# Batch 0 of a tuned attention and gating kernel: q loaded like k and transposed by TensorE, statistics of v summed beside ScalarE's copies, and a new written order

## The chip, the cores and the metric

The kernel runs on one core of a Trainium2 chip. Its time is the device time of one execution, in microseconds (us), and the median of several runs is what is compared. The profile and the trace come from one further execution under the hardware profiler, whose own time and span are in the table below. The engines are called as in the profile: PE (TensorE), DVE (VectorE), ACT (ScalarE), POOL (GpSimd) and SP, the queue that issues every transfer here.

## What is computed

```python
def _attn_ref(q, k, v, phi):                     # q, k, v: 8 x 8 x 576 x 64, phi: 8 x 8 x 576 x 32
    a = np.exp(phi - np.max(phi, axis=2, keepdims=True))
    a = a / (np.sum(a, axis=2, keepdims=True) + 1e-09)
    k_m = np.einsum('bhsm,bhsd->bhmd', a, k)
    v_m = np.einsum('bhsm,bhsd->bhmd', a, v)
    scores = 1.0 / np.sqrt(64) * np.matmul(q, k_m.transpose(0, 1, 3, 2))
    attn = np.exp(scores - np.max(scores, axis=-1, keepdims=True))
    attn = attn / (np.sum(attn, axis=-1, keepdims=True) + 1e-09)
    return np.matmul(attn, v_m)

def _moe_ref(x, w_in, w_spatial, b_spatial, w_out):   # x: 8 x 576 x 512, heads side by side
    h = np.maximum(x @ w_in, 0.0)
    u, v = h[..., :512], h[..., 512:]
    mu = np.mean(v, axis=-1, keepdims=True)
    var = np.mean((v - mu) ** 2, axis=-1, keepdims=True)
    v_n = (v - mu) / np.sqrt(var + 1e-06)
    v_s = np.einsum('ts,bsd->btd', w_spatial, v_n) + b_spatial[None, :, None]
    return (u * v_s) @ w_out
```

The weights of the second half come as 64-bit floats, which the kernel turns into 32-bit ones with integer operations ("decoding" below).

## The kernel before, in words

The eight batches are worked off one after the other, each as a set of stages that overlap with those of the next batch. Every stage is a Python generator, and each `yield` ends one step of it. Two strings set the order in which the steps are written: `START` for the weights and the beginning of batch 0 and batch 1, `PLAN` for one round of the steady state. A letter names the stage, the digit its part, a prime the batch ahead, `*2` a repetition. Since the order is written out by hand (`manual_schedule`), every engine works its own instructions off in that order, and an instruction that waits holds up all that stand behind it on its engine.

The stages of a batch: `P` (`memory_weights`) loads phi, takes column maxima (`half`, `mx`, `cm`), the exponential and the sums `es`. `K` (`memories`) loads k and v into `kv_sb`, multiplies them with the exponentials (`kvm`), divides (`den`, `kmn`, `vmn`) and transposes (`tk`, `tv`, `kT`, `vT`). `Q` (`queries`) loads q and makes `qT`. `S` (`scores`) makes the scores `sc`, brings them to rows with four VectorE transposes (`sm`), takes the softmax, turns it back (`aT`) and splits it into a rounded high part `ah` and a rest `al`. `M` (`products`) makes v_m times one half of `w_in` (`mp`; `M0` for u, `M1` for v) and splits it into `mh` and `ml`. `U` (`units`, tile `pu`) and `V` (`gate`, tile `pv`) multiply `ah`, `al` with `mh`, `ml`; `V` also normalizes v and splits it into `vh`, `vl`. `G` (`spatial`, tile `ps`) and `O` (`project`, tile `po`) are the two large multiplications behind.

The stages of the weights: `D` loads `w_in` in eight transfers (`raw`), `L0`, `L1` decode the half for u and `E0`, `E1` the half for v, each in two tiles of 128 rows by twice 512 words. `W`, `T`, `B` load `w_spatial` and its bias, transpose it into `wt` and split it into `wth`, `wtl` (and `ws1`, `ws2` for the last 64 rows). `X0` to `X3` load and decode `w_out`.

The set `ON_VECTOR` says what VectorE does. A `.add` or `.mul` of a decoding that is not in it goes to GpSimd in two instructions of 512 words each (for `.add`, with a conversion on ScalarE ahead). A rest (`ml...`, `wtl...`) that is not in it is made by a matmul with minus the identity into the same bank and a ScalarE copy; one that is in it is a VectorE subtraction. A name `es3` stands for the sums `es` of batch 3, on VectorE if it is in the set and on GpSimd if not.

Before the change q of every batch comes in pieces of 32 numbers (128 bytes) that lie so in the tile that four VectorE transposes of 32x32 blocks make `qT` of them. Means and variances of v are taken by VectorE's `bn_stats` and `bn_aggr`, and GpSimd makes 1/sqrt(var) and the shift of them.

## Time and profile before

| | before |
|---|---|
| median of 3 runs | 435.25 us (434.84 to 436.11) |
| profiled execution, its own time | 435.84 us |
| its span, first to last instruction | 434.1 us |
| PE busy | 400.4 us, 92% of the span |
| PE weight loads (beside the matmuls) | 333.1 us, 77% |
| DVE busy | 294.9 us, 68% |
| ACT busy | 223.0 us, 51% |
| POOL busy | 74.0 us, 17% |
| mean granted clock of TensorE | 0.971 |

An engine's busy share is an average over the start, in which transfers and decoding keep the engines waiting for each other, and a long stretch in which TensorE works without a break. The clock is given as a share of full speed: 1.00 is 2.4 GHz, 0.50 is 1.2 GHz.

### The profile page before, as it was taken

How to read it: one execution, taken by the hardware profiler on the slowest of the kernel's cores; microseconds unless marked ns; L12 is line 12 of the kernel's file. 1: busy time of each engine (PE TensorE's matmuls, PEld its weight loads, DVE VectorE, ACT ScalarE, POOL GpSimd, SP SyncE). 2: the span in 40 equal slices, each digit the busy share in tenths (PEclk: the TensorE clock that was granted, in tenths of full speed). 3: DMA queues.
4: the chain of work that ended last, by engine and by line, in shares of the span. 5: the costliest groups of instructions: out<-in, count | busy, mean ns of one | idle time of the engine just before them, and what ended most of it. 6: DMA issues, size and time to landing. Idle time of an engine off the chain costs nothing.

```text
span 434.1 us, 9211 instructions
## 1 busy us (share of the span) xinstructions
PE 400.4 (92%) x3815; PEld 333.1 (77%) x3815; DVE 294.9 (68%) x546; ACT 223.0 (51%) x427; POOL 74.0 (17%) x148
## 2 busy tenths in 40 slices
...
GB/s 292 405 192 360 123 57 99 271 0 149 208 181 2 72 179 210 47 24 113 204 142 2 112 176 203 16 73 132 210 68 24 98 2 2 2 74 23 2 2 121
DMA packets 94543, 50.69 MB, mean 117 GB/s; under 512 B 75491, under 2 KB 79587, under 8 KB 94501
## 3 DMA queue, kind: packets, MB, share of 16 engines
q1 hardware_dynamic: 94500, 50.10, 47.5%
...
## 4 chain that ended last, share of the span: by engine, by line
PE 87%; DVE 6%; DMA 4%; ACT 1%; issue 1%; SPq 0%; DVEq 0%; ACTq 0%
PE ps L634 28%; PE po L674 23%; PE pv L547 13%; PE pu L596 12%; PE kvm L371 4%; PE mp L517 4%; DMA raw<-in_moe_w_in_dram 2%; DMA w_rem<-in_moe_w_spatial_dram 2%; PE sc L455 2%; DVE power L206 1%; DVE win_sb L214 1%; DVE win_sb L219 1%; DVE qT L441 1%; DVE half L317 0%; DVE g L645 0%
## 5 line engine op out<-in xcount | busy, mean ns | idle before, releaser
L634 PE MATMUL ps<-wth,vh 128*128 128x288 f32 x256 | 57.8, 307 | 0.1
L559 POOL TENSOR_SCALAR rs<-mv 128x1 f32<-128x1 f32 (+1 forms) x40 | 10.1, 253 | 262.7 <-DVE mv L556 238.0
L634 PE MATMUL ps<-wth,vl 128*128 128x288 f32 x256 | 54.6, 295 | 0.0
L634 PE MATMUL ps<-wtl,vh 128*128 128x288 f32 x256 | 54.5, 294 | 0.0
L674 PE MATMUL po<-wol,gh 128*128 128x512 f32 x128 | 50.8, 397 | 0.0
L674 PE MATMUL po<-woh,gh 128*128 128x512 f32 x128 | 50.6, 395 | 0.0
L674 PE MATMUL po<-woh,gl 128*128 128x512 f32 x128 | 50.2, 392 | 0.0
L680 ACT COPY o<-po 128x512 f32<-128x512 f32 x36 | 21.2, 588 | 55.8 <-PE po L674 53.5
L634 PEld LDWEIGHTS ps<-wth,vh 128*128 128x128 f32 x256 | 40.4, 188 | 10.9 <-issue 5.9
L554 DVE BATCH_NORM_STATS2 st<-vr 128x6 f32<-128x512 f32 (+1 forms) x40 | 27.3, 682 | 29.8 <-ACT vr L551 29.6
L656 ACT CAST gh<-g 128x512 fp32r<-128x512 f32 x32 | 19.1, 620 | 49.1 <-DVE g L645 49.1
L634 PEld LDWEIGHTS ps<-wtl,vh 128*128 128x128 f32 x256 | 41.2, 188 | 0.0
L634 PEld LDWEIGHTS ps<-wth,vl 128*128 128x128 f32 x256 | 41.0, 188 | 0.0
L605 ACT ACTIVATE u<-pu 128x576 f32<-128x576 f32 x32 | 20.2, 659 | 30.6 <-PE pu L596 30.2
L569 ACT ACTIVATE vr<-vr,sh,rs 128x512 f32<-128x512 f32 (+1 forms) x40 | 31.9, 817 | 5.4 <-POOL sh L564 5.4
L547 PE MATMUL pv<-mh,al 128*128 128x512 f32 (+1 forms) x80 | 31.6, 395 | 0.0
L547 PE MATMUL pv<-mh,ah 128*128 128x512 f32 (+1 forms) x80 | 31.6, 395 | 0.0
L547 PE MATMUL pv<-ml,ah 128*128 128x512 f32 (+1 forms) x80 | 31.6, 395 | 0.0
L658 DVE TENSOR_TENSOR grl<-g,grh 128x64 fp32r<-128x64 f32 x32 | 6.7, 213 | 36.3 <-ACT grh L656 36.3
L645 DVE TENSOR_TENSOR g<-u,ps 128x576 f32<-128x576 f32 x32 | 24.1, 752 | 9.7 <-PE ps L634 9.5
L596 PE MATMUL pu<-ah,mh 128*128 128x288 f32 x128 | 29.2, 309 | 0.0
L371 PE MATMUL kvm<-kv_sb,phi_sb 64*32 64x128 f32 x1152 | 23.3, 300 | 5.8 <-DMA kv_sb<-in_v_dram 5.0
...
## 6 DMA issues: line engine op xcount, KB each, us to landing
...
```

What stands on the lines that cost most here:

```text
L371: nc.tensor.matmul(kvm[r][32 * j : 32 * j + 32], phi_sb[halves[r], j, i, :], kv_sb[halves[r], j, :, i * D : (i + 1) * D], start=(i == 0), ...
L517: nc.tensor.matmul(mps[r][32 * j : 32 * j + 32, :], vT[D * r : D * r + D, 32 * j : 32 * j + 32], win_sb[D * r : D * r + D, j, cs], start=True,
L547: nc.tensor.matmul(pv, x[:, r, cs], m[:, r, DM:DFF], start=(n == 0), stop=(n == 5))
L554: nc.vector.bn_stats(st6, vr)
L569: nc.scalar.activation(vr, vr, AF.Identity, bias=sh, scale=rs)
L596: nc.tensor.matmul(pu[:, hf, 0:HALF], m[:, r, cs], a[:, r, hf * HALF : (hf + 1) * HALF], start=(n == 0), stop=(n == 5),)
L605: nc.scalar.activation(u[:, dt, :].rearrange("p (a s) -> p a s", a=2), pu[:, :, 0:HALF], AF.Relu)
L634: nc.tensor.matmul(ps[:, hf, 0:HALF], a, w[:, hf * HALF : (hf + 1) * HALF], start=(n == 0), stop=(n == len(ops) - 1),)
L645: nc.vector.tensor_tensor(g.rearrange("p (a s) -> p a s", a=2), u[:, dt, :].rearrange("p (a s) -> p a s", a=2), ps[:, :, 0:HALF], op=ALU.mult,
L656: nc.scalar.copy(hi, x)
L674: nc.tensor.matmul(po, a, w, start=(n == 0), stop=(n == 11))
L680: nc.scalar.copy(o, po)
```

## The change

Five things change. The first three are in batch 0 alone.

- q of batch 0 is loaded by one transfer in the layout of k (rows of 9 times 64 numbers, 2,304 bytes in one piece). TensorE transposes it in 24 pieces into five banks (`tq_0` to `tq_4`), and ScalarE copies these into `qT` with six instructions. VectorE's four transposes of batch 0 are gone.
- The columns of the scores of batch 0 come in another sequence by that, so the way back (`aT`) takes eight VectorE transposes in place of four, with a stride in what they write.
- v of batch 0: the ScalarE instruction that applies Relu also sums (`accum_out`); GpSimd makes plus and minus the mean of the sum; a ScalarE Square with minus the mean as bias sums the squares, and GpSimd makes variance, root and shift of it. `bn_stats` and `bn_aggr` of batch 0 are gone.
- `ON_VECTOR` is another set: `E0.mul`, `E1.add`, `E1.mul` go to GpSimd (and ScalarE), `L1.add`, `L1.mul` come to VectorE; the rests of `w_spatial` are named one by one, and some are now made by a matmul; the sums `es` of batches 4 to 7 go to GpSimd.
- `START` and `PLAN` are written in another order.

```diff
 START = """
-    D1 P W T3 P T3 B D0 T3 D0 T3 P*2 D1 T3 T2 L0 P E0 D1 T2*2 P T2 T3*2 P K P E0*2 L0 D1 P*2 K
...
+    W B T1 B P W P T1*2 W P D0 P T0 P*2 D0 P*2 T1 L0 P L0*2 W D0 D1 P L0 D0 D1 K L1*2 E0 P*2 K
...
 ON_VECTOR = set(
     """
-    es0 E0.add E0.mul E1.add E1.mul L0.add L0.mul ml000 wtl2 X0.add X1.add X1.mul X3.wol ml110
-    ml111 ml100 ml101 es2 es3 es4 es5 es6 es7
+    es0 E0.add ml010 L0.add L0.mul L1.add L1.mul wtl00 wtl0512 wtl1512 X0.add X0.mul X0.wol
+    X1.add X1.mul X2.add X2.wol ml111 ml100 ml101 es2 es3
     """.split()
...
-            tensor.matmul(x, minus, hi, start=False, stop=True, skip_group_check=True)
+            n = x.shape[0]
+            tensor.matmul(
+                x, minus[0:n, 0:n], hi, start=False, stop=True, skip_group_check=True
+            )
...
-                yield from low(f"wtl{si}" if cs.start == 0 else None, wtl[:, si, cs], part, hi)
+                yield from low(f"wtl{si}{cs.start}", wtl[:, si, cs], part, hi)
             else:
-                yield from low(None, ws2[0:SR, cs], part[0:SR], hi[0:SR])
+                yield from low(f"wtl{si}{cs.start}", ws2[0:SR, cs], part[0:SR], hi[0:SR])
...
     def queries(b, _):
+        if b == 0:
+            q_sb = one.tile([P, NJ, NX * D], F32, tag="q_sb", name="q_all")
+            nc.sync.dma_start(
+                q_sb, q[b].rearrange("(j r) (p i) d -> (r p) j (i d)", r=2, i=NX)
+            )
+            yield
+            qT = state["qT", b] = one.tile([P, H, HALF], F32, name="qT")
+            for j in range(NJ):
+                tq = bank(f"tq_{j}")
+                for n in range(4):
+                    cs = slice(n * P, (n + 1) * P)
+                    nc.tensor.transpose(tq[:, cs], q_sb[:, j, cs], ident)
+                yield
+                nc.scalar.copy(
+                    qT[:, 2 * j : 2 * j + 2, 0:256].rearrange("p r (i s) -> p r i s", s=64),
+                    tq.rearrange("p (i r s) -> p r i s", r=2, s=64),
+                )
+                yield
+            tq = bank("tq_4")
+
+            for j in range(NJ):
+                cs = slice(j * P, (j + 1) * P)
+                nc.tensor.transpose(tq[:, cs], q_sb[:, j, 7 * D :], ident)
+                nc.tensor.transpose(tq[0:D, cs], q_sb[:, j, 8 * D :], ident)
+            yield
+            for c in range(2):
+                rows = slice(D * c, D * c + D)
+                nc.scalar.copy(
+                    qT[rows, :, 256:],
+                    tq[rows].rearrange("p (h s) -> p h s", s=64)[:, :, 32 * c : 32 * c + 32],
+                )
+                yield
+            return
...
+                if b == 0:
+                    to = aT[:, r].rearrange("p (h x i) -> p i h x", x=32, i=NX)
+                    nc.vector.transpose(
+                        to[:, c:8:2], sm[:, r, c, 0:8].rearrange("p (i h) m -> p i h m", h=2)
+                    )
+                    nc.vector.transpose(to[:, 8, c], sm[:, r, c, 8])
...
+        if b == 0:
+
+            nc.scalar.activation(vr, pv, AF.Relu, accum_out=sums[:, 0:1])
+            yield
+            nc.gpsimd.tensor_scalar(sums[:, 1:2], sums[:, 0:1], -1.0 / DM, None, op0=ALU.mult)
+            nc.gpsimd.tensor_scalar(mv[:, 0:1], sums[:, 0:1], 1.0 / DM, None, op0=ALU.mult)
+            squares = vh[:, st, :] if st < NI else t1[0:SR]
+            nc.scalar.activation(
+                squares, vr, AF.Square, bias=sums[:, 1:2], accum_out=sums[:, 2:3]
+            )
+            yield
+            nc.gpsimd.tensor_scalar(
+                rs, sums[:, 2:3], 1.0 / DM, 1e-6, op0=ALU.mult, op1=ALU.add
+            )
+        else:
...
```

The built programs show where these instructions land. The first place is the queue of transfers (SP) from its start to the second phi, before:

```order
L174 DMA raw<-in_moe_w_in_dram 128x1024
L326 DMA phi_sb<-in_phi_dram 128x4x288
L256 DMA w_sb<-in_moe_w_spatial_dram 128x4x576
L257 DMA w_rem<-in_moe_w_spatial_dram 64x576
L259 DMA b_sb<-in_moe_b_spatial_dram 1x576 x2
L174 DMA raw<-in_moe_w_in_dram 128x1024 x4
L359 DMA kv_sb<-in_k_dram 128x4x576
L174 DMA raw<-in_moe_w_in_dram 128x1024
L359 DMA kv_sb<-in_v_dram 128x4x576
L174 DMA raw<-in_moe_w_in_dram 128x1024 x2
L432 DMA q_sb<-in_q_dram 32x72x32 x4
L326 DMA phi_sb<-in_phi_dram 128x4x288
```

And in the changed kernel:

```order
L260 DMA w_sb<-in_moe_w_spatial_dram 128x4x576
L261 DMA w_rem<-in_moe_w_spatial_dram 64x576
L263 DMA b_sb<-in_moe_b_spatial_dram 1x576 x2
L330 DMA phi_sb<-in_phi_dram 128x4x288
L178 DMA raw<-in_moe_w_in_dram 128x1024 x6
L363 DMA kv_sb<-in_k_dram 128x4x576
L363 DMA kv_sb<-in_v_dram 128x4x576
L434 DMA q_all<-in_q_dram 128x4x576
L178 DMA raw<-in_moe_w_in_dram 128x1024 x2
L330 DMA phi_sb<-in_phi_dram 128x4x288
```

`w_spatial` moved to the front, the four strided transfers of q became one, and the last two of the eight `raw` (those of `E1`) now stand behind q. Six `raw`, `w_spatial`, phi and k stand ahead of v in both.

The second place is TensorE from the transposes of batch 0's memories (`tk`) to its scores (`sc`), before:

```order
L283 MATMUL wt_308<-ident,w_dup 128x128 x4
L283 MATMUL wt_308<-ident,w_rem_dup 128x64
L411 MATMUL tk_317<-ident,kmn 128x128 x2
L416 MATMUL tv_325<-ident,vmn 128x128
L283 MATMUL wt_338<-ident,w_sb 128x128 x4
L283 MATMUL wt_338<-ident,w_rem 128x64
L455 MATMUL sc_0_0_344<-qT,kT 32x288
```

And in the changed kernel, where the eight pieces of `tq_4` end with six more like the last two rows, and the scores follow:

```order
L415 MATMUL tk_295<-ident,kmn 128x128 x2
L443 MATMUL tq_300<-ident,q_all 128x128 x4
L420 MATMUL tv_307<-ident,vmn 128x128
L443 MATMUL tq_312<-ident,q_all 128x128 x4
L159 MATMUL wt_190<-wth,minus 128x512
L443 MATMUL tq_324<-ident,q_all 128x128 x4
L443 MATMUL tq_332<-ident,q_all 128x128 x4
L454 MATMUL tq_338<-ident,q_all 128x128
L455 MATMUL tq_338<-ident,q_all 64x128
```

The transposes of q came in between `tk` and the scores, and two of the five transposes of `w_spatial` moved behind the scores.

The third place is VectorE around the reading of batch 0's scores, before:

```order
L206 SCALAR_TENSOR_TENSOR power<-raw,power 128x1024
L441 STREAM_TRANSPOSE qT<-q_sb 128x576 x4
L315 TENSOR_TENSOR half<-phi_sb 128x512
L317 TENSOR_TENSOR half<-half 128x4x64
L319 TENSOR_TENSOR mx<-half 128x128
L466 STREAM_TRANSPOSE sm<-sc_0_0_344 128x288
L466 STREAM_TRANSPOSE sm<-sc_0_1_345 128x288
L466 STREAM_TRANSPOSE sm<-sc_1_0_346 128x288
L466 STREAM_TRANSPOSE sm<-sc_1_1_347 128x288
L321 TENSOR_TENSOR mx<-mx,phi_sb 128x128
L472 TENSOR_REDUCE rmx<-sm 128x36
```

And in the changed kernel:

```order
L319 TENSOR_TENSOR half<-phi_sb 128x512
L321 TENSOR_TENSOR half<-half 128x4x64
L503 STREAM_TRANSPOSE sm<-sc_0_0_350 128x288
L323 TENSOR_TENSOR mx<-half 128x128
L503 STREAM_TRANSPOSE sm<-sc_0_1_351 128x288
L325 TENSOR_TENSOR mx<-mx,phi_sb 128x128
L503 STREAM_TRANSPOSE sm<-sc_1_0_352 128x288
L503 STREAM_TRANSPOSE sm<-sc_1_1_353 128x288
L341 TENSOR_REDUCE cm<-mt_382 128x2
L509 TENSOR_REDUCE rmx<-sm 128x36
L210 SCALAR_TENSOR_TENSOR power<-raw,power 128x1024
L512 TENSOR_TENSOR sm<-sm,rmx 128x1152
```

The four transposes of q are gone, fewer decoding steps stand ahead of the scores, and one of them (L210 of `E1`, L206 before) now stands inside the softmax.

## Rows read from the trace of the kernel before

**Rows 1.** Windows: start:end, us; busy us (instructions) by engine; PE clock; DMA share, GB/s.

```profile
0.00:57.44 57.44, 27.65 (x422) 16.37 (x422) 42.77 (x67) 27.79 (x50) 14.05 (x20) 0.79 0.95 259
57.77:434.10 376.33, 372.46 (x3394) 316.41 (x3392) 251.79 (x480) 194.89 (x378) 59.91 (x128) 1.00 0.41 95
```

**Rows 2.** Windows of 5 us inside the start; columns as in rows 1.

```profile
40.00:45.00 5.00, 3.48 (x35) 1.16 (x36) 4.93 (x9) 0.00 (x0) 3.20 (x3) 0.50 1.13 346
...
55.00:60.00 5.00, 5.00 (x133) 4.85 (x114) 4.91 (x14) 3.62 (x7) 0.15 (x1) 0.78 0.20 45
```

**Rows 3.** Timeline of DVE: start us, us, instruction, count [idle before].

```profile
29.66 1.21 DVE L206 SCALAR_TENSOR_TENSOR power<-raw,power 128x1024 int32<-128x1024 int32 x1
...
35.18 2.32 DVE L206 SCALAR_TENSOR_TENSOR power<-raw,power 128x1024 int32<-128x1024 int32 x1
37.43 2.75 DVE L441 STREAM_TRANSPOSE qT<-q_sb 128x576 f32<-128x576 f32 x4
...
43.35 1.56 DVE L466 STREAM_TRANSPOSE sm<-sc 128x288 f32<-128x288 f32 x4
...
51.44 0.68 DVE L162 TENSOR_TENSOR ws<-wt,ws 64x512 fp32r<-64x512 f32 x1
...
55.12 0.74 DVE L499 TENSOR_TENSOR al<-aT,ah 128x576 fp32r<-128x576 f32 x1
```

**Rows 4.** Timeline of PE in the start.

```profile
23.41 2.39 PE L371 MATMUL kvm<-kv_sb,phi_sb 64*32 64x128 f32 x80 [5.01 <-DMA kv_sb<-in_v_dram]
25.73 0.80 PE L157 MATMUL wt<-wth,minus 128*128 128x512 f32 x1
...
27.35 0.29 PE L383 MATMUL kvm<-ones,es 64*32 64x2 f32 x16
...
36.08 1.06 PE L283 MATMUL wt<-ident,w_sb 128*128 128x128 f32 x4
...
38.34 4.02 PE L455 MATMUL sc<-qT,kT 64*32 64x288 f32 x32 [0.91 <-DVE qT L441]
...
53.51 3.85 PE L371 MATMUL kvm<-kv_sb,phi_sb 64*32 64x128 f32 x135 [0.82 <-ACT ml L160]
...
57.77 0.42 PE L596 MATMUL pu<-ah,mh 128*128 128x288 f32 x2
```

**Rows 5.** Windows of 2 us around the end of the last `raw` transfers; columns as in rows 1.

```profile
22.00:24.00 2.00, 0.59 (x24) 0.62 (x32) 2.00 (x5) 2.00 (x3) 0.00 (x0) 1.00 1.04 392
...
26.00:28.00 2.00, 1.65 (x81) 1.12 (x81) 2.00 (x3) 1.44 (x2) 0.00 (x0) 1.00 0.84 127
```

**Rows 6.** Groups by line: shapes, count | busy us, mean ns of one | idle before.

```profile
L569 ACT ACTIVATE vr<-vr,sh,rs 128x512 f32<-128x512 f32 (+1 forms) x40 | 31.9, 817 | 5.4 <-POOL sh L564 5.4
...
L551 ACT ACTIVATE vr<-pv 128x512 f32<-128x512 f32 (+1 forms) x40 | 23.2, 594 | 8.4 <-PE pv L547 8.3
...
L398 ACT ACTIVATE kmn<-kvm,den 128x128 f32<-128x128 f32 x16 | 5.7, 362 | 0.5 <-DVE den L394 0.5
```

**Rows 7.** Timeline of POOL in the start.

```profile
34.80 3.84 POOL L212 TENSOR_TENSOR win_sb<-win_sb,raw 128x512 f32<-128x512 f32 x2 [32.35 <-ACT raw L204]
...
40.21 3.07 POOL L222 TENSOR_TENSOR win_sb<-win_sb,power 128x512 f32<-128x512 f32 x2
```

**Rows 8.** Chain that ended last: start us, us, engine, tile, line, count.

```profile
57.93 1.59 PE pu L596 x12
59.52 2.80 PE pv L547 x12
...
71.60 1.13 PE sc L455 x32
72.73 1.78 PE ps L634 x12
74.51 1.88 PE mp L517 x32
...
106.62 0.99 PE kvm L371 x58
```

More of the change, by code (lines that the diff above doesn't have):

```diff
@@ new lines @@
+    L1*3 L0 P L1 Q T0 T1 E0 T1 L1 T1 T0 P E0 P D1 E0*3 D1 T0 T2 E0 T0 K L1 K*2 L0 K*3 W T2 L0 K
+    L0 Q E1 K*2 Q*2 K Q P' T2 E0 Q T0 E1 T2 Q*5 T0 Q S P'*2 S P' S P' S*2 E1 P'*2 S T4 T2 E1*2
+    T2 T4 M0 X1 E1 P' M0 P' S E1 T2 K' P' M0 T4 S K' T3 T4 X0 E1 M1 T4 M0*2 Q' T3 P' S M1 T4 M0
+    P' S*3 T3 M0 M1 S K' M1*2 S T3 S*2 T4 T3 P'*2 M1 T3 U3 S T3 U2 Q' P' X1 M1 X0 K' S*2 X0 X1
+    V0 X1 X0*2 K'' U2 X0 K' X1 K' X1 V0 K' U2 V0 X0 X1 X0 V1*2 K' X0 P'' U3 V2 V0 U3 V0 K'*2 X1
+    V2 V1 Q' K' V0 U0 V2 V1 V4 V1 V0 X0 V1 Q'*2 K' V1 Q' U0 V4 U0 U1 V3 U1 V3 U1 V2 G1 V4 V2 X0
@@ L39 @@
+    X1 S' G1 V3 S' X3 V2 V4*2 G0 S'*2 V4 M1' V3 S' V4 V3*2 S' M0' G0 V2 G1 M1' X3 V4 M0' X3*2 V3
+    X3 S' G0 G1 P'' G0 M0' G1 X1*2 S' X3 X2 S' G2 G1 G0*2 G1 M1' P'' G1 G0 G2 M1' X3 G3 P'' G2
+    G1 X2 P'' K'' G3 X2*2 G0 G2 M0'*2 G2 P'' M1' P'' X2*2 G2 G3 P'' M0' G0 X2 O1 P'' X3*3 G3 X2
+    M1' M0' X2*2 P'' G3*2 X2 O3 X3 M1' G2 O2 O0 G3 S'*2 O3 S'*2 O2 O3 Q'' S'*4 O2 P'' G2 S'*2
+    P'' G3 O0 O3 O1 O2 G3 O0 G2 P''*2 O0 O1*2 P''
 """
 PLAN = """
-    P'*4 K' U0 V1 V0 K' U0 V2 U0 K' U2 V0 V1 U1 V1 V0 V2 V1 V2 K' V0 V4 U1 V1 V3 Q' K' V0 P'' V1
@@ L48 @@
+    V3 U3 Q' U2 V1 V4*2 K' V2 P'' K'*2 P'' V3 P'' K' P'' V3 V4 K' K'' U3 K' S' U2 U3 V2 V4 S' V3
+    S' V3 S'*2 G0 V4 G1 P'' M0' Q'' P'' M1' M0' S' V3 V2 S' M1'*2 G0 V4 G1 G0 V3 S' G1 V4 G0 P''
+    M1' S' M0' Q G1 G0 M1' G0 S' G1 S' M1' K'' P'' G0 S' Q'' G1 G0*2 M0' G2 G3 P'' G2 S' G3 G1*3
+    G2 G3 G2*3 M1' G3 O3 G2 S' G3 S'*2 O0 G3 S' O1 G3 O0 S' G3 P'' M0' S' O3 O0 G2 O0 G3 O1 O3
+    M0' O3 O4 G2 Q'' O2 M0' O1 O4 O1 V0' O2 O4*2 Q'' O2 V0' O2
 """
@@ L492, in scores @@
             for c in range(2):
[L493 to L495 removed]
+                if b == 0:
[5 more added lines that the diff above has]
+                else:
+                    nc.vector.transpose(
+                        aT[:, r].rearrange("p (i c x) -> p c i x", c=2, x=32)[:, c], sm[:, r, c]
+                    )
                 yield
```

37 lines of the change are left out of this document (8 added, 29 removed).

## The prediction

> **What bounds the kernel now.** I read the windows first, then the timelines of TensorE and VectorE in the start, then the chain. The reader is to see two regimes. From 57.77 us on TensorE is busy for 372.46 of the 376.33 us that are left, at full clock [rows 1], and what it does there are matmuls that the change does not touch. So the time is: the moment at which TensorE reaches its first `pu` matmul with all inputs there, plus the work that is left then. Up to 57.44 TensorE is busy for only 27.65 us, and VectorE for 42.77 [rows 1]; in the windows VectorE is full from 40 on while TensorE idles or runs at half clock [rows 2]. What ends last there is VectorE's queue. It decodes weights, makes the four transposes of q at 37.43, gets to the scores at 43.35 and to the first rest `al` at 55.12 [rows 3]. The scores themselves waited for those transposes: `sc` starts at 38.34 after an idle time that L441 ended [rows 4]. TensorE's first `pu` at 57.77 comes 2.65 behind `al`, because 135 `kvm` matmuls of batch 1 stood ahead of it at half clock, from 53.51 for 3.85 us [rows 4].
>
> So the question is when the scores of batch 0 are ready for VectorE, and how much VectorE does from there to `al`.
>
> **The start, step by step.** *Transfers.* Before v stand the same bytes in both orders, so v lands at 23.4 as now, where `kvm` starts [rows 4]. Behind it q, 1.18 MB, needs 3.0 us at the 392 GB/s of the window before the strided q and 9.3 at the 127 GB/s of the window in it [rows 5]. k and v, in the same layout, are the nearest rows: I take 3.0, so q is there at 26.4. Nothing asks for it before 28.7 (below), so its transfer is hidden; at the slow rate it would land at 32.7. The last two `raw` follow it, about 1.0 MB or 2.7 us more, at 29.1; VectorE comes to them (L187) later than that.
>
> *Memories.* The `kvm` group ran from 23.41 to 27.64, with an L157 matmul of 0.80 inside [rows 4] that is elsewhere now: 27.2. VectorE's `den` and two ScalarE `kmn` of 0.36 [rows 6] give `tk` at about 28.7.
>
> *Transposes of q.* Two queues run side by side. On ScalarE there stand, from `kmn` to the last q copy, six full-width copies (four of q, one `wth`, one `wtl`) and nine smaller ones. The copies of q write with a stride that no row shows; I price them as L551, 0.59, and the small ones as `kmn`, 0.36 [rows 6]: 27.9 + 6 x 0.59 + 9 x 0.36 = 34.7. On TensorE four groups of four transposes cost 1.06 each by the group of `wt` at 36.08 (half clock), one L157 0.80, and the eight of `tq_4` two groups [rows 4]: 28.7 + 4.2 + 0.8 + 2.1 = 35.8, and two copies of 0.36 behind: 36.5. At full clock TensorE is well ahead, and ScalarE's 34.7 decides. I take 35.4 for the first score matmul. Half of the scores cost 0.6 at full clock (1.13 for all [rows 8]) and twice that at half: VectorE reads them at 36.2, in place of 43.35. Bounds: 35.3 and 37.7.
>
> VectorE itself is free at about the same time. Behind `den` it has three decoding steps of 1.21 and five short ones, at most 0.68 each like the L162 [rows 3]: 27.7 + 3.6 + 3.4 = 34.7, or 37.3 if the two GpSimd operations of `E0.mul` shut it out for 1.3 each (below).
>
> *From the scores to `al`.* Before this took 55.12 - 43.35 = 11.8 us without a gap [rows 3]. Now one L206 of 1.21 comes in (the decoding step of `E1`), a subtraction L162 of 0.68 goes [rows 3], and the first `aT` pair becomes four transposes that write with a stride; I take 0.1 for it, and up to 0.7 if short pieces cost twice their share: 12.4. GpSimd comes on top. Its two additions at 34.80 took 3.84 us [rows 7], and the L206 that VectorE began at 35.18 took 2.32 in place of 1.21: as if it had stood still to 36.3, inside the pair, and then run [rows 3]. Now four such GpSimd operations of `E1` fall between the scores and `al`, and two VectorE instructions there read two SBUF tiles, L210 and L512. Each can lose one GpSimd operation, (3.84 - 1.21) / 2 = 1.3 without the lockout, so the bounds are 0 and 2.6. I take 1.6: 1.1 for L210, as before, and 0.5 for L512. So `al` starts at 36.2 + 12.4 + 1.6 = 50.2.
>
> That is also about when the other inputs come. `E1` now goes through ScalarE (behind the q copies: 35.4, three conversions of 1,024 words, each about twice a copy of 0.59, 38.8), GpSimd (3.84 + 3.07 [rows 7], 45.7), the last `mp` matmuls (a quarter of 32 that take 1.88 at full clock [rows 8], 0.9 at half), an `mh` copy of 0.59 and the hand-overs, 47.5; VectorE wants that `mh` for `ml`, just ahead of `al`, at 49.6. Cover: 2.1 us. If GpSimd is later than that, everything behind `ml` is late one for one.
>
> *First `pu`.* TensorE's queue has ahead of it 80 `kvm` matmuls of batch 1 (3.85 for 135 at half clock [rows 4], so 2.3), from the exponential of phi at about 48 (on ScalarE it is the sixth instruction behind that of the scores), and a last L157 that waits for three ScalarE instructions behind `ah`: 51.2. Before: 57.77.
>
> **The sum.** 51.2, plus the 376.33 left from the first `pu` on [rows 1], plus what moved behind it: the other 64 `kvm` matmuls and the sums, 1.1 (0.99 for 58 [rows 8]), and one rest of batch 1 by matmul, 0.25. The clock: before it is 0.50 up to 55 and 0.78 on average from 55 to 60 [rows 2], so it rose behind the `kvm` run that began at 53.51. Now that run begins at about 48 and I expect the rise between 51 and 53; at half clock the first `U` halves cost double (1.59 for two [rows 8]): 0.8, between 0 and 1.6. For small waits later 0.3. Sum 430.0 against the span of 434.1, 4.1 less. The profiled execution took 435.84, 1.7 more than its span, and lies 0.6 above the runs' median; 435.25 - 4.1 = **431.1**.
>
> **What I cost at nothing.** *Statistics.* Five `bn` pairs leave VectorE, which is no gain by itself: it is not what TensorE waits for there. ScalarE gets five Squares; with a bias they lie between L551's 0.59 and L569's 0.82 [rows 6], and the sums may add 0.2 to ten instructions. GpSimd makes five small operations per block in place of three. The cover: from the first ScalarE Relu, at 56.0, to the last `vh` stand 30 instructions, near 19 us by these rows and 16 as they overlap: 72.1. TensorE needs that `vh` after four `U`, five `V`, six pieces of `ps`, `sc` and `mp`: 6.4 + 7.0 + 4.8 + 1.1 + 1.9 [rows 8] and 1.5 for the rest behind 51.2 + 0.8, 74.7. Slack 2.6; without it, each us late costs one. *Transfers of batch 1.* Its q shares the tile of batch 0's q and waits for `tq_4` at 35.4 instead of VectorE at 40.2. *PLAN.* TensorE's rows of batches 1 to 7 come in almost the same order; `es4` to `es7` go to GpSimd, busy for 59.91 of 376.33 us [rows 1], two batches ahead of their use. If that cover failed, a batch would lose about two operations of 512 words, 3 us [rows 7].
>
> **Rivals.**
> - *`E1` is late.* The chain above breaks its 2.1 us of cover, because q's copies stand ahead of it on ScalarE and GpSimd is shut out too. Needs 5 us of lateness to eat 2.8 us of the gain: 434.0 to 436. Against it: GpSimd's four rows now sum to 6.9 with lockouts in them. 0.11.
> - *Statistics late.* ScalarE or GpSimd lose the 2.6 us of slack and 1 to 3 more: 432.5 to 434. For it: L569 waited 5.4 us for GpSimd's `sh` in all [rows 6], and GpSimd now has more to do ahead of it. 0.14.
> - *More is gained.* Scores at 35.3, no lockout, clock up at once: 36.2 - 35.3 + 1.6 + 0.8 = 3.3 less at the most, 427.8 to 429.3. 0.13.
> - *Slower: GpSimd shuts VectorE out.* Place: between the scores and `al`. By rows `E1`'s four GpSimd operations take 6.9 us, and `es` of batch 1 begins there too, some 3 us more. If VectorE stood for all 9.9 instead of 1.6, the time is 431.1 + 8.3 = 439.4; it is slower than before by over 0.3% from 7.1 of the 9.9 on. For it: the doubled L206. Against it: the transposes of q at 37.43 ran at 0.69 each beside GpSimd's pair, without such a jump, and most of the softmax reads one tile or a bank. 0.07. The Trainium skill has the rule behind it (SBUF — State Buffer, § Who interferes with whom): the port pair that VectorE and GpSimd share is locked for a whole instruction, and the loser blocks. The 2.32 us of L206 agrees with that.
>
> **How the numbers follow.** The forecast as summed, 429.3 to 432.5, has 0.55. A difference of 0.3% (1.3 us) is about what this measurement can tell from none: same is 433.9 to 436.6. Faster: 0.55 + 0.14 + 0.13 = 0.82; same 0.11; slower 0.07. The range leaves out the slow rival (0.07), most of late `E1` (0.09) and the end of the gain (0.04): 428.3 to 434.3.
>
> **What would show it.** In the new trace: v lands near 23.4 and q before 29; `tk` near 28.7; the scores' VectorE transposes near 36 with an idle time ahead of them that TensorE ends; L210 stretched by GpSimd; `al` near 50; the first `pu` near 51; no gap of TensorE behind that. I am wrong if `pu` comes after 55, if ScalarE's q copies cost much more than 0.6, if `ml` ahead of `al` waits for `mh`, or if TensorE waits for `vh` in the first `ps`.

## The result, and the profile after

The changed kernel takes 428.92 us (median of 4 runs, 428.77 to 429.15) against 435.11 (434.84 to 436.11) for the kernel before: a ratio of 0.986 with a 95% interval of 0.983 to 0.988, so 6.2 us or 1.4% faster. The profiled execution took 428.77, and its span is 427.0; before it was 434.1. Windows of it, cut at the first `pu`, with the columns of [rows 1]:

```profile
0.00:48.15 48.15, 25.34 (x370) 15.73 (x371) 36.44 (x56) 29.76 (x57) 16.64 (x21) 1.00 1.02 309
48.15:427.00 378.85, 374.69 (x3475) 320.42 (x3475) 246.42 (x462) 201.49 (x395) 70.02 (x153) 1.00 0.40 95
```

The first `pu` comes at 48.15 in place of 57.77 [rows 1], 9.6 us earlier. What is left from there on is 378.85 in place of 376.33, 2.5 more. The difference is the 7.1 us that the span lost. The gain lies in the start, and what moved behind it takes a part back. Where the profile has TensorE's clock in it (from 26.5 on) it is full, 1.00; the mean up to the first `pu` was 0.79 before [rows 1].

VectorE in the start, from a timeline:

```profile
26.79 0.23 DVE L397 TENSOR_SCALAR den<-kvm 128x1 f32<-128x1 f32 x2 [1.38 <-PE kvm L387]
27.05 0.17 DVE L398 RECIPROCAL den<-den 128x2 f32<-128x2 f32 x1
27.13 1.71 DVE L210 SCALAR_TENSOR_TENSOR power<-raw,power 128x1024 int32<-128x1024 int32 x1
...
33.56 0.47 DVE L503 STREAM_TRANSPOSE sm<-sc 128x288 f32<-128x288 f32 x1
...
36.89 1.43 DVE L210 SCALAR_TENSOR_TENSOR power<-raw,power 128x1024 int32<-128x1024 int32 x1
38.24 2.44 DVE L512 TENSOR_TENSOR sm<-sm,rmx 128x1152 f32<-128x1152 f32 x1
...
47.30 0.76 DVE L543 TENSOR_TENSOR al<-aT,ah 128x576 fp32r<-128x576 f32 x1 [0.22 <-ACT ah L541]
```

VectorE reads the scores at 33.56 (before 43.35 [rows 3]) without an idle time ahead of it, and gets to `al` at 47.30 (before 55.12). So 7.8 of the 9.6 us lie ahead of `al`. The other 1.8 lie between `al` and the first `pu`, 2.65 before [rows 3, 4] and 0.85 now: 135 `kvm` matmuls at half clock, 3.85 us of them, stood ahead of that `pu` [rows 4], and now 78 take 1.36 at full clock and are done when `al` begins (below). L512 takes 2.44, where the same step took 1.35 in the run below that has no GpSimd work beside it: GpSimd's additions of `E1` run from 35.94.

TensorE from the memories to the first `pu`, and ScalarE between the memories and the scores:

```profile
27.73 0.59 PE L415 MATMUL tk<-ident,kmn 128*128 128x128 f32 x2 [1.12 <-ACT kmn L402]
28.15 0.60 PE L443 MATMUL tq<-ident,q_all 128*128 128x128 f32 x4
...
32.09 1.59 PE L492 MATMUL sc<-qT,kT 64*32 64x288 f32 x32 [0.80 <-ACT qT L459]
...
45.97 1.36 PE L375 MATMUL kvm<-kv_sb,phi_sb 64*32 64x128 f32 x78 [0.54 <-ACT ml L164]
...
48.15 0.51 PE L654 MATMUL pu<-ah,mh 128*128 128x288 f32 x2
```

```profile
27.31 0.63 ACT L402 ACTIVATE kmn<-kvm,den 128x128 f32<-128x128 f32 x2 [3.92 <-DVE den L398]
...
29.73 0.60 ACT L445 COPY qT<-tq 128x512 f32<-128x512 f32 x1
30.21 0.60 ACT L164 CAST wtl<-wt 128x512 fp32r<-128x512 f32 x1
30.69 1.09 ACT L445 COPY qT<-tq 128x512 f32<-128x512 f32 x2
31.64 0.79 ACT L459 COPY qT<-tq 64x256 f32<-64x256 f32 x2
```

Four transposes take 0.60 here, at full clock, in place of the 1.06 of [rows 4] at half. TensorE is ahead of ScalarE, and the scores start at 32.09, behind the first of ScalarE's last two q copies (the second ends at 32.43).

### The profile page after: what moved, and what is told of

It is laid out like the page before. It is cut to its first block, busy times and chain, and to the rows that moved or that the text cites. A ratio compares the mean times of both kernels' runs of the same rounds, so it can differ in the third digit from the quotient of the medians.

```text
span 427.0 us, 9272 instructions
## 1 busy us (share of the span) xinstructions
PE 400.0 (94%) x3844; PEld 336.2 (79%) x3844; DVE 282.9 (66%) x517; ACT 231.2 (54%) x452; POOL 86.7 (20%) x173
## 4 chain that ended last, share of the span: by engine, by line
PE 85%; DVE 7%; DMA 3%; ACT 3%; issue 1%; POOL 0%; SPq 0%; ACTq 0%
PE ps L692 29%; PE po L732 23%; PE pv L591 12%; PE pu L654 10%; PE kvm L375 4%; PE mp L561 3%; PE sc L492 2%; DMA raw<-in_moe_w_in_dram 2%; DMA w_rem<-in_moe_w_spatial_dram 1%; DVE power L210 1%; ACT vr L599 1%; DVE sm L512 1%; DVE win_sb L218 1%; DVE aT L532 1%; DVE power L187 0%
## 5 line engine op out<-in xcount | busy, mean ns | idle before, releaser
L615 DVE BATCH_NORM_STATS2 st<-vr 128x6 f32<-128x512 f32 (+1 forms) x35 | 24.0, 687 | 50.7 <-ACT vr L612 50.7
L732 PE MATMUL po<-woh,gh 128*128 128x512 f32 x128 | 50.4, 394 | 0.0
L732 PE MATMUL po<-woh,gl 128*128 128x512 f32 x128 | 50.4, 394 | 0.0
L732 PE MATMUL po<-wol,gh 128*128 128x512 f32 x128 | 50.4, 393 | 0.0
L618 POOL TENSOR_SCALAR few<-few 128x1 f32<-128x1 f32 (+1 forms) x35 | 9.3, 266 | 161.7 <-DVE few L616 157.9
L627 ACT ACTIVATE vr<-vr,few 128x512 f32<-128x512 f32 (+1 forms) x40 | 32.4, 814 | 1.7 <-POOL few L622 1.4
L591 PE MATMUL pv<-mh,ah 128*128 128x512 f32 (+1 forms) x80 | 33.0, 412 | 0.0
L632 DVE TENSOR_TENSOR vl<-vr,vh 128x512 fp32r<-128x512 f32 x32 | 21.8, 680 | 11.8 <-ACT vh L630 11.7
L732 PEld LDWEIGHTS po<-woh,gl 128*128 128x128 f32 x128 | 24.0, 188 | 5.6
L612 ACT ACTIVATE vr<-pv 128x512 f32<-128x512 f32 (+1 forms) x35 | 20.7, 593 | 14.1 <-PE pv L591 14.1
```

The source lines that it names most:

```text
L591: nc.tensor.matmul(pv, x[:, r, cs], m[:, r, DM:DFF], start=(n == 0), stop=(n == 5))
L612: nc.scalar.activation(vr, pv, AF.Relu)
L615: nc.vector.bn_stats(st6, vr)
L627: nc.scalar.activation(vr, vr, AF.Identity, bias=sh, scale=rs)
L632: nc.vector.tensor_tensor(vl[:, st, :], vr, vh[:, st, :].bitcast(F32), op=ALU.subtract)
L732: nc.tensor.matmul(po, a, w, start=(n == 0), stop=(n == 11))
```

## The experiments

The theory after this result: the time is the first `pu` plus a constant; the first `pu` follows `al`; and `al` follows a chain from the sums of batch 0 over `den`, ScalarE's copies and the scores to VectorE's softmax, beside which VectorE's own queue is about as late. The rivals: the new order and the set alone give the gain; the transfer of q is hidden and worth nothing; the clock that TensorE keeps is the cause and not a consequence; the statistics contribute.

All runs in one table. Each ratio is to runs of the kernel before that were taken together with the run in question; the median of these lay between 434.46 and 435.90, so it is the ratios, and not the medians, that compare across the rows. "First pu" and "left" (span less first pu) are from the traces, one execution each. Those of "82 idle matmuls" (438.61), "E0.mul and E1 on VectorE" (435.09) and "20 idle matmuls" (431.77) took 1.1, 4.0 and 0.9 us more than the median of their runs.

| run | median us | ratio to before, 95% | first pu | left |
|---|---|---|---|---|
| before | 435.11 | 1 | 57.77 | 376.3 |
| changed | 428.92 | 0.986 (0.983 to 0.988) | 48.15 | 378.9 |
| changed, q as before | 435.55 | 1.003 (1.001 to 1.005) | 55.14 | 378.6 |
| changed, q fetched in 128-byte pieces | 432.69 | 0.995 (0.993 to 0.997) | 51.64 | 379.0 |
| before, with the new q alone | 434.53 | 0.999 (0.998 to 1.001) | 56.93 | 376.6 |
| changed, statistics as before | 428.88 | 0.986 (0.984 to 0.989) | 48.57 | 378.5 |
| before, 82 idle matmuls | 437.51 | 1.006 (1.004 to 1.008) | 60.48 | 376.3 |
| before, 25 idle matmuls | 435.49 | 1.001 (1.000 to 1.003) | 57.33 | 376.4 |
| changed, E0.mul and E1 on VectorE | 431.10 | 0.991 (0.989 to 0.993) | 51.88 | 381.4 |
| changed, L210 ahead of den | 430.56 | 0.991 (0.989 to 0.993) | 49.37 | 378.8 |
| the same and two casts moved | 431.65 | 0.993 (0.991 to 0.996) | 50.99 | 378.8 |
| changed, E0.mul in the idle time, casts moved | 429.31 | 0.988 (0.985 to 0.990) | 48.05 | 378.9 |
| changed, 20 idle matmuls | 430.91 | 0.991 (0.988 to 0.993) | 50.29 | 379.7 |
| changed, 29 idle matmuls | 432.90 | 0.993 (0.991 to 0.994) | 52.31 | 378.9 |

The last column is the first finding: 376.3 to 376.6 in the old order, 378.5 to 379.0 in the new one, in all runs but two (381.4, explained below, and 379.7, left open). Within one order, what a run costs or gains it does ahead of the first `pu`. No run takes the new order and the new set `ON_VECTOR` apart, and none puts only the old `PLAN` back; what each of them gives is not shown.

### q as before in the new order, and only its transfer slow

The first run takes the new `queries` out, and `aT` with it; `START` gets one more `Q` step, so that the transfers of q are issued at the same place:

```diff
-        if b == 0:
-            q_sb = one.tile([P, NJ, NX * D], F32, tag="q_sb", name="q_all")
...
-            return
         q_sb = one.tile([P, H, NX, 32], F32, name="q_sb")
```

> The changed kernel with q of batch 0 as before: four strided transfers (issued at the same place in SP's queue) and four VectorE transposes; all else as changed. If VectorE's queue is what ends last (my reading): q comes about 9 us after v (at 32.7), the transposes take 2.75 us of VectorE and wait for it, and the last two raw come behind q at about 35, so scores and al are 3 to 4.5 us later than in the changed kernel: 432 to 433.5. If the order and the set ON_VECTOR alone give the gain: within 0.5 of 428.9. If it is the clock that TensorE keeps by the transposes of q: the clock falls to half in the start as before, and the time is above 433.5.

The second keeps TensorE's transposes and fetches the same tile in short pieces:

```diff
-            nc.sync.dma_start(
-                q_sb, q[b].rearrange("(j r) (p i) d -> (r p) j (i d)", r=2, i=NX)
-            )
+            for j in range(NJ):
+                for g in range(2):
+                    cs = slice(32 * g, 32 * g + 32)
+                    nc.sync.dma_start(
+                        q_sb[:, j].rearrange("p (i d) -> p i d", i=NX)[:, :, cs],
+                        q[b, 2 * j : 2 * j + 2].rearrange("r (p i) d -> (r p) i d", i=NX)[:, :, cs],
+                    )
```

> The changed kernel with q of batch 0 in the same layout in the tile and transposed by TensorE, but fetched in pieces of 128 bytes (eight transfers), as slow as before's. If the transfer matters: q is complete at about 32.7 in place of 26.4, TensorE's transposes and the last two raw behind q (wanted by VectorE at 31.16) come 4 to 5 us late: 432.5 to 434. If the faster transfer is hidden anyway and only the freed VectorE counts: within 0.5 of 428.9.

With q as before the gain is gone: 435.55, above the 432 to 433.5 that I expected of VectorE, and where I had placed the rival of the clock, which did fall (0.98 in the mean). So the new order and the set by themselves give no gain: the first `pu` is 2.6 earlier and 2.2 more is left behind it. With only the transfer slow it is 432.69, as expected for "the transfer matters". By spans, 433.7, 430.6 and 427.0: with q in short pieces either way, taking it out of VectorE is worth 3.1 us in this order, and the long pieces another 3.6. (The 3.1 are not VectorE's own time alone: 1.5 of them come from the next `raw` behind q, for which L187 runs at 35.98 instead of 34.52 in the rows below.) VectorE in the run with the slow transfer, then in the run with q as before:

```profile
34.52 0.69 DVE L187 TENSOR_SCALAR power<-raw 128x1024 int32<-128x1024 int32 x1 [3.34 <-DMA raw<-in_moe_w_in_dram]
...
50.80 0.76 DVE L547 TENSOR_TENSOR al<-aT,ah 128x576 fp32r<-128x576 f32 x1 [0.22 <-ACT ah L545]
```

```profile
33.48 0.78 DVE L445 STREAM_TRANSPOSE qT<-q_sb 128x576 f32<-128x576 f32 x1 [2.19 <-DMA q_sb<-in_q_dram]
35.98 0.70 DVE L187 TENSOR_SCALAR power<-raw 128x1024 int32<-128x1024 int32 x1 [1.72 <-DMA raw<-in_moe_w_in_dram]
36.59 2.09 DVE L445 STREAM_TRANSPOSE qT<-q_sb 128x576 f32<-128x576 f32 x3
```

It is not q itself that is waited for in the first of them (its scores start at 32.96, 0.9 later than in the changed kernel), but the last two `raw` of `w_in` that stand behind q in the queue: VectorE waits 3.34 us for them, and `al` is 3.5 later, the whole price. With q as before, VectorE waits 2.19 for q and 1.72 for `raw` and works 0.78 + 2.09 on the transposes, 6.8 in all. The scores are read at 40.36 in place of 33.56, 6.8 later. VectorE's rows alone account for it: TensorE made the scores at half clock there (0.50 from 32 to 40), but VectorE read them without an idle time ahead, so that up to `al` nothing is left for the clock. My 3 to 4.5 had taken the waits to lie inside each other. What the run does not tell is how the new order would do with q in a better place for a slow transfer.

### The new q in the old order

The kernel before gets the new `queries` and `aT`, and as many more `Q` steps in `START` as it has yields:

```diff
-    E0 Q K E1 P' L1 K L0 T2 L1 T1 E1 L1*2 K W E1 T4 K*2 L1 Q*3 K Q K'*2 P' K*2 P' T0 S P' S T0
+    E0 Q K E1 P' L1 K L0 T2 L1 T1 E1 L1*2 K W E1 T4 K*2 L1 Q*3 K Q*7 K'*2 P' K*2 P' T0 S P' S T0
```

> The kernel before with only the q of batch 0 changed: loaded like k, transposed by TensorE in 24 pieces, six ScalarE copies; old order and old ON_VECTOR. VectorE's queue is full from 20.37 to 55 there, so the four transposes (2.75 us) go out of it: the scores are read 2 to 2.75 us earlier, and the time is 432.4 to 433.2 against 435.1. If the copies on ScalarE and half-clock transposes stand in the way instead (sc behind 41): no change. If q's part were the whole gain: 429 to 430.

No measurable gain: 0.999 (0.998 to 1.001). The transposes did leave VectorE, and the scores are read at 42.47 in place of 43.35, 0.9 earlier and not 2.75. Windows of this run (TensorE alone: us, busy, clock, DMA share, GB/s) and VectorE's timeline:

```profile
33.44:40.26 6.82, 5.32 (x24) 0.50 0.94 357
```

```profile
37.30 1.77 DVE L315 TENSOR_TENSOR half<-phi_sb 128x512 f32<-128x512 f32 x1
39.11 1.51 DVE L317 TENSOR_TENSOR half<-half 128x256 f32<-128x256 f32 x1
40.66 1.24 DVE L319 TENSOR_TENSOR mx<-half 128x128 f32<-128x128 f32 x1
42.47 1.58 DVE L499 STREAM_TRANSPOSE sm<-sc 128x288 f32<-128x288 f32 x4 [0.57 <-PE sc L488]
```

Two things took it back. L315, which took 0.65 at 40.10 before, now lies beside GpSimd's work of 34.65 to 43.04 and takes 1.77. And the scores are late: 20 of the 24 transposes run at half clock, behind `tk`, which the old order only reaches at 35.24. So the new q is worth next to nothing in the old order and 6.7 us, by spans, in the new one. The two parts carry the gain together.

### The statistics

```diff
-        if b == 0:
-
-            nc.scalar.activation(vr, pv, AF.Relu, accum_out=sums[:, 0:1])
...
-        else:
```

> The changed kernel with the statistics of v of batch 0 by VectorE's bn_stats and bn_aggr again; all else as changed. If the statistics are not on the path (slack of about 1.4 us at the first ps, VectorE not waited for there): 428.6 to 429.4, the same as the changed kernel. If VectorE is the bound behind the start too: five pairs of near 1 us each come back, 431 to 433.

The same as the changed kernel, 428.88. In the changed kernel ScalarE pays for each sum with an instruction of its own:

```profile
52.74 0.60 ACT L599 ACTIVATE vr<-pv 128x512 f32<-128x512 f32 x1
53.24 0.19 ACT L599 ACTIVATION_READ_ACCUMULATOR vr<-pv 128x1 f32 x1
...
54.11 0.73 ACT L604 ACTIVATE vh<-vr,few 128x512 fp32r<-128x512 f32 x1
54.73 0.21 ACT L604 ACTIVATION_READ_ACCUMULATOR vh<-vr,few 128x1 f32 x1
```

The last `vh` begins at 69.84 and the `ps` matmul that needs it at 71.82. The slack is there, about 1.4 us, and neither version uses it up.

### Is it the clock?

Idle matmuls of the identity, whose result nothing reads, were put into the idle times of TensorE in the kernel before, in unused columns of banks:

```diff
+        if b == 0:
+            for _ in range(40):
+                nc.tensor.matmul(kvb[1][:, 256:384], ident, ident, start=True, stop=True)
```

(the same behind the scores and behind `mb`, 24 and 18 times)

> The kernel before with 82 matmuls of the identity by itself put into three idle times of TensorE in the start (40 behind the first kvm sums, 24 behind the scores, 18 behind mb), into unused columns of banks; they compute nothing that is used. They should keep the granted clock up. If the clock is only a consequence and VectorE ends last: TensorE waits for al (57.34 to 58.1) anyway, so 434.4 to 435.2, 0.7 gained at most. If the half clock itself cost the time before: 2 us or more gained, below 433.

> The kernel before with fewer idle matmuls of the identity than in the first such run (11 behind den, 8 behind the scores, 6 behind mb; each takes 0.26 us or twice that, not 0.11), so that no wanted instruction should stand behind them by more than a few tenths. They compute nothing that is used. If the half clock in the start is only a consequence: 434.0 to 435.2, as before or up to 0.7 less. If the half clock is a cost by itself: below 433.5.

The first missed its mark: such a matmul runs in two passes (80 records for 40), and the 40 took 10.54 us, not 4.4, so that the wanted `wt`, `tk` and scores stood behind them. That made the scores late (42.45 in place of 38.34 [rows 4]), but VectorE still read three of the four at 43.78, only 0.4 later than before [rows 3]. What held it were the 24 idle matmuls behind the scores, which write into the bank of the fourth: VectorE waited 4.27 us for it, and `al` came at 59.57, 4.45 late.

```profile
30.01 10.54 PE L401 MATMUL kvm<-ident 128*128 128x128 f32 x80 [1.12 <-DVE den L397]
...
57.95 2.12 PE L375 MATMUL kvm<-kv_sb,phi_sb 64*32 64x128 f32 x135 [0.37 <-ACT ml L160]
...
60.48 0.42 PE L606 MATMUL pu<-ah,mh 128*128 128x288 f32 x2
```

```profile
49.24 0.48 DVE L476 STREAM_TRANSPOSE sm<-sc 128x288 f32<-128x288 f32 x1 [4.27 <-PE sc L471]
```

The second (11, 8 and 6 of them) held a mean clock of 0.99 in place of 0.97 and gained nothing: 1.001 (1.000 to 1.003). TensorE was at full clock from about 33 to 53, and still the scores were read at 43.40 and `al` came at 54.80 (43.35 and 55.12 before [rows 3]). So up to `al` the half clock of the old order costs next to nothing: VectorE does not wait for TensorE there.

Behind `al` it does cost something, and the second run could not tell, since its clock was at half again from 54 on and its `kvm` took 3.42. In the first run the same 135 `kvm` matmuls ran at full clock, in 2.12 us instead of 3.85, and the first `pu` came 0.91 behind `al` instead of 2.65, with the same 376.3 left. By these rows about 1.7 us of the old kernel's time are the half clock between `al` and the first `pu`; that is an estimate, since no run changed this alone, and more than the 0.7 at most that I had allowed. The clock is thus a consequence of the order up to `al` and a cost by itself behind it.

In the new order TensorE's clock counts ahead of `al` too, since VectorE and the scores are nearly level there, as the next two runs show. One VectorE step was moved ahead of `den`, and in a second run two ScalarE casts of `w_spatial` also went behind the q copies:

```diff
-    L1*3 L0 P L1 Q T0 T1 E0 T1 L1 T1 T0 P E0 P D1 E0*3 D1 T0 T2 E0 T0 K L1 K*2 L0 K*3 W T2 L0 K
+    L1*3 L0 P L1 Q T0 T1 E0 T1 L1 T1 T0 P E0 P D1 E0*3 D1 T0 T2 E0 T0 K L1 K L0 K*4 W T2 L0 K
```

> The changed kernel with one VectorE step moved: the first L210 behind den (27.13, 1.71 us) now stands ahead of den, where VectorE is idle for 1.38 us. If VectorE's queue alone ends last up to the scores: VectorE is 1.3 us earlier, al 1.3 earlier, 427.6. If the scores (sc at 32.09, its first half 32.9) are as late as VectorE, which was ready at 33.56: 0.6 gained at most, 428.3 to 428.9. If neither (E1's GpSimd chain to ml sets al): no change.

```diff
-    L0 Q E1 K*2 Q*2 K Q P' T2 E0 Q T0 E1 T2 Q*5 T0 Q S P'*2 S P' S P' S*2 E1 P'*2 S T4 T2 E1*2
+    L0 Q E1 K*2 Q*2 K Q P' E0 Q T0 E1 Q*5 T0 Q T2 S P'*2 S P' S P' S*2 E1 T2*2 P'*2 S T4 T2 E1*2
```

(the line above it in `START` also loses one `T2` at its end)

> As the run with L210 moved, and two ScalarE casts of w_spatial (wth, wtl, 0.5 us each, and the TensorE rest between them) moved from among the q copies to behind them. Then the scores too come about 1.1 us earlier, and E1's conversion 0.6 earlier. If VectorE and the scores together set al: 427.4 to 428.0, more than the move of L210 alone. If E1's chain through ScalarE and GpSimd is the next bound, al waits for ml: at most 0.6 gained, 428.3 or more.

Both were slower than the changed kernel, against every line of what I expected. The trace of the first says why:

```profile
25.45 2.29 DVE L210 SCALAR_TENSOR_TENSOR power<-raw,power 128x1024 int32<-128x1024 int32 x1
27.67 0.21 DVE L397 TENSOR_SCALAR den<-kvm 128x1 f32<-128x1 f32 x2
...
34.14 0.48 DVE L503 STREAM_TRANSPOSE sm<-sc 128x288 f32<-128x288 f32 x1 [0.53 <-PE sc L492]
```

L210 did not fit into the 1.38 us: beside GpSimd's `E0.mul` it took 2.29, so `den` came 0.88 later, and ScalarE and the scores (32.96) with it. `al` (48.53) is 1.23 later; the other 0.4 is a longer wait for `ah` (0.60 in place of 0.22), behind TensorE's `mp`, which ran at a clock of 0.50 from 44 to 46. VectorE now waits for the scores. In the changed kernel the two queues were within 0.3 us of each other: here VectorE reads 1.18 behind the start of `sc`, there that would be 33.27, and it came at 33.56.

In the second run TensorE idled 2.72 us ahead of `tk` (1.12 in the changed kernel) and fell to half clock. Windows of the same stretch, of the changed kernel and of this run, with the columns of [rows 1]:

```profile
28.35:31.76 3.41, 2.94 (x26) 2.63 (x24) 3.37 (x4) 3.41 (x10) 0.00 (x0) 1.00 0.99 290
```

```profile
28.35:31.76 3.41, 3.11 (x15) 3.04 (x16) 3.38 (x3) 2.58 (x9) 0.58 (x1) 0.50 1.05 391
```

15 matmul passes in place of 26, and ScalarE waits for them (busy 2.58 of 3.41): the scores start at 33.79, 0.8 later than in the run before it, although two casts had left ScalarE's queue ahead of them. Its time, 431.65, is near the 431.1 of the prediction, which had priced half-clock transposes, but that is no test of the sum: its scores start at 33.79, not at the 35.4 forecast, and 0.9 of its delay is L519, which took 1.04 beside GpSimd (0.18 without).

### Could it be faster still?

`E0.mul` on VectorE, in the idle time ahead of `den`, with the casts moved; and the `.mul`, `.add` of `E1` on VectorE as well, where the order has them:

```diff
-    es0 E0.add ml010 L0.add L0.mul L1.add L1.mul wtl00 wtl0512 wtl1512 X0.add X0.mul X0.wol
+    es0 E0.add E0.mul ml010 L0.add L0.mul L1.add L1.mul wtl00 wtl0512 wtl1512 X0.add X0.mul X0.wol
...
-    L1*3 L0 P L1 Q T0 T1 E0 T1 L1 T1 T0 P E0 P D1 E0*3 D1 T0 T2 E0 T0 K L1 K*2 L0 K*3 W T2 L0 K
+    L1*3 L0 P L1 Q T0 T1 E0 T1 L1 T1 T0 P E0 P D1 E0*3 D1 T0 T2 E0 T0 K L1 K E0 K L0 K*3 W L0 K
```

(and the `T2` steps moved as above)

> The changed kernel with E0.mul on VectorE, inside its idle 1.38 us ahead of den (so that GpSimd does nothing beside the L210 of 27.13, which should fall from 1.71 to 1.21), and with the ScalarE casts wth, wtl of w_spatial and the rest between them behind the q copies instead of among them. If VectorE sets al and TensorE keeps its clock: scores read 0.5 earlier, 428.2 to 428.5. If den is pushed back by the extra VectorE step, everything is late by as much: 429 to 430. If TensorE falls to half clock in its idle time ahead of tk, as in the run with both moves: above 430.

```diff
-    es0 E0.add ml010 L0.add L0.mul L1.add L1.mul wtl00 wtl0512 wtl1512 X0.add X0.mul X0.wol
+    es0 E0.add E0.mul E1.add E1.mul ml010 L0.add L0.mul L1.add L1.mul wtl00 wtl0512 wtl1512 X0.add X0.mul X0.wol
```

> The changed kernel with E0.mul, E1.add and E1.mul on VectorE again (ON_VECTOR), so that no GpSimd decoding runs in the start. If VectorE's queue ends last: E0.mul (1.2) fits into VectorE's idle 1.38 ahead of den, E1's two operations add 2.4 between the scores and al, and 1.3 of stretching by GpSimd goes, so al comes 1.0 to 2.4 later: 430 to 431.3. If the shared use costs more than the work (lockout theory): faster than the changed kernel, 427 to 428.5.

The first is 429.31, not told apart from the changed kernel. By the number alone that is the branch of a late `den`, but `den` came earlier (26.55 against 26.79). Its own rows:

```profile
24.10 2.35 DVE L223 TENSOR_TENSOR win_sb<-win_sb,power 128x1024 f32<-128x1024 f32 x2
26.55 0.23 DVE L397 TENSOR_SCALAR den<-kvm 128x1 f32<-128x1 f32 x2
...
26.89 1.21 DVE L210 SCALAR_TENSOR_TENSOR power<-raw,power 128x1024 int32<-128x1024 int32 x1
...
32.80 0.48 DVE L503 STREAM_TRANSPOSE sm<-sc 128x288 f32<-128x288 f32 x1
...
42.32 1.04 DVE L519 TENSOR_SCALAR rsum<-rsum 128x36 f32<-128x36 f32 x1
```

The step went in without cost, L210 fell from 1.71 to 1.21, and the scores are read at 32.80, 0.76 earlier. Then a 0.18 instruction (L519) takes 1.04 beside the last multiplication of `E1` on GpSimd (until 43.33), L512 takes 2.45 as before, and `al` at 47.20 is only 0.1 earlier. With all of `E1` on VectorE, L512 is back at 1.35:

```profile
39.90 1.35 DVE L512 TENSOR_TENSOR sm<-sm,rmx 128x1152 f32<-128x1152 f32 x1
```

but two operations of 1.22 each come in, and from the scores (35.44) to `al` (50.93) it is 15.5 in place of 13.7. It ends at 431.10, inside what I expected: what VectorE loses beside GpSimd is less than the work that GpSimd takes off it. (Its profiled execution was the longest of its runs, 435.09. VectorE waited longer for `raw` in it, 1.22 and 0.83 us against 0.59, so a part of the late scores is not the step of `E0`. And TensorE waited 2.7 us just ahead of `pu`, the granted clock was 0.63 from 51.88 to 60, and that is why 381.4 are left in the table.)

Last, idle matmuls in the changed kernel, ahead of `kvm` of batch 0, which takes 4.1 us there from 22.46, at half clock by the 2.22 that it takes below:

```diff
         nc.tensor.transpose(mb, cmb.rearrange("s r p -> s (r p)"), ident)
+        if b == 0:
+            for _ in range(20):
+                nc.tensor.matmul(mtb[:, 256:384], ident, ident, start=True, stop=True)
```

> The changed kernel with 20 idle matmuls of the identity put into TensorE's 8 us of idle time ahead of 20.94, into unused columns of a bank; they compute nothing that is used. The kvm run of batch 0 (144 at half clock from 22.46 to 26.5, 4.1 us) should then run at full clock, about 2.5 us. If den, the ScalarE chain behind it and VectorE's queue set al, as I now think: den at about 25.4 in place of 26.79, VectorE loses its idle 1.38, but its L210 then lies beside GpSimd's multiplications: al 0.5 to 1.3 earlier, 427.6 to 428.4. If GpSimd takes all of it back: 428.9.

> As the run with 20 idle matmuls, but 29 of them, so that TensorE stays busy until about 20.5 and the clock should not fall ahead of kvm; they compute nothing that is used. If den, the ScalarE chain and VectorE set al, and the half clock in the transposes of q was what took the gain away in the run with 20: kvm in 2.5 us, den near 25.4, sc near 31, al 0.5 to 1.3 earlier than in the changed kernel, 427.6 to 428.5. If the clock falls in the transposes again: 430 or more. If GpSimd's multiplications beside L210 and L218 push VectorE back by as much: 428.9.

Both were slower, the second by more. `kvm` did get to full clock with 29 of them (2.22 us), and then TensorE stood still. TensorE's timeline with 29, then with 20:

```profile
22.72 2.22 PE L379 MATMUL kvm<-kv_sb,phi_sb 64*32 64x128 f32 x143 [0.40 <-DMA kv_sb<-in_v_dram]
...
28.92 0.31 PE L391 MATMUL kvm<-ones,es 64*32 64x2 f32 x14 [3.96 <-issue]
```

```profile
28.90 0.69 PE L447 MATMUL tq<-ident,q_all 128*128 128x128 f32 x2 [0.95 <-issue]
```

"issue" means that no semaphore held it. The two runs stop at different instructions of the program, but behind the same number of them: 222 matmul records stand ahead of either gap, and both go on at 28.9. That points to the supply of further instructions, of which the fillers use up a part; no row names it, so it is argued. The changed kernel has done 187 by then and does not meet the gap. By the end of the gap the clock had fallen to half again, and the scores came at 35.86 and 33.77.

## Why the prediction was right, and where it was off

The direction, the range and the outline of the mechanism were right: 431.1 (428.3 to 434.3) against 428.92. The size was not: the change in the span was 7.1, and I had summed 4.1. The measured time lies outside the forecast as summed (429.3 to 432.5) and inside the rival *More is gained* (427.8 to 429.3), to which I gave 0.13. Of that rival's three conditions two held, earlier scores (33.56, before 35.3) and the clock up at once; the third, VectorE undisturbed by GpSimd, did not (1.3 us in all). By the prediction's own steps:

*The start of the chain.* v and `den` were forecast for 23.4 and 27.7; measured 22.46 and 26.79. (27.64 less the 0.80 of L157 is 26.8, not the 27.2 that I wrote.) `tk` 28.7 against 27.73. q landed at 25.3 and was wanted at 28.15: hidden, as said.

*The scores, the step that failed.* I had 35.4 for the first score matmul and 36.2 for VectorE's reading; it was 32.09 and 33.56. Two sizes were wrong in it. ScalarE's 15 copies were added up by their durations, 6.8 us; they took 5.1, from 27.31 to 32.43, because each begins about 0.12 before the one ahead of it ends (0.60 long, 0.48 apart): 1.7 of the 3.3, and 0.6 more because `den` was early. Another 0.7 is the clock: TensorE's transposes were costed at half of it, 1.06 for four, and I put the scores 0.7 behind ScalarE for that; they ran at full clock, 0.60, and so did everything behind. The last 0.3 is that the scores start behind the first of the last two copies. VectorE's own queue, forecast for 34.7, was ready at 33.56 and then set the reading: the idle time ended by TensorE, which I had named as a sign, did not come. The overlap is a general mistake in sums of busy time: the distance of two starts is the price, not the duration. The Trainium skill (ScalarE: Activation LUTs, § What ACT_TABLE_LOAD costs) says that back-to-back ACTIVATEs overlap by about 93 ns, which the trace shows a little larger. Here it is 0.12 us, between copies and casts. So 2.6 of the 3.0 us that the sum was too long lie here.

*From the scores to `al`.* 14.0 forecast, 13.74 measured, with L210 stretched by 0.2 and L512 by 1.1 where I had 1.1 and 0.5. The Trainium skill (SBUF — State Buffer, § Who interferes with whom) has it that a VectorE instruction with two SBUF inputs contends with a GpSimd instruction that reads SBUF; the runs agree: L210 takes 1.21 with GpSimd idle and 2.29 beside `E0.mul`.

*`E1`.* Its chain was in time: the last `mh` that VectorE's `ml` needs began at 44.85, and `ml` ran at 46.43 without a wait. The cover was about 1 us, in place of 2.1.

*The rest.* First `pu` 51.2 against 48.15, and behind it 378.8 against 378.85. That agreement is luck in part: the 0.8 for a half clock there did not come, and TensorE was busy for 2.2 us more behind the first `pu` (374.69 against 372.46), of which I had priced 1.35. My reading of the clock before was too simple, too: it was not at half all the way up to 55, but at full from about 47 to 50.4, and fell again. That the 135 `kvm` at half clock made the first `pu` late there is borne out by the run with 82 idle matmuls.

*What I cost at nothing.* The statistics: right, though the slack was 1.4 and not 2.6; by [rows 8] six pieces of `ps` are 5.3 and not 4.8, which makes the slack forecast 3.1. The order of the later batches: no run tests it alone, and it only fits the sum. The transfer of q: right for the change as it stands, but I had not seen what the cover was worth. With short pieces 3.6 us come back, through the `raw` behind q and not through q.

*The half clock.* The three runs whose clock fell in the transposes of q (L210 and casts moved, 20 and 29 idle matmuls) ended at 430.9 to 432.9, each with other delays beside it. That the clock stays up in the changed kernel is shown, and so is what a half-clock stretch does to the scores. Why it stays up is not settled: TensorE idled 1.1 us ahead of `tk` there, 2.05 in the run with L210 moved alone, where the clock stayed up too, and 2.7 in the run where it fell, but no run set the clock without moving something else.
